# Attention output as full-array matmuls, with new buffer, load and filler orders, in a fused attention and FFN kernel on one Trainium2 core

## The chip, the cores and the metric

The kernel runs on one core of one Trainium2 chip. The metric is the device time of one execution in microseconds (us), as a median of several. All executions in this document are of the fast state. A profiled span is mostly 1.7 to 2.2 us shorter than the time reported for the same execution (2.7 for the profile of the kernel before, 3.2 at most), so spans are compared with spans and times with times. Several chips were used; each kernel was timed beside the kernel before on its own chip.

## The reference

Linear attention for 8 batches of 8 heads (576 tokens, head size 64), then a feed-forward layer on all 4608 tokens.

```python
q_s = exp(q - max(q, -1)); q_s = q_s / (sum(q_s, -1) + 1e-09)   # over head_dim
k_s = exp(k - max(k, 2));  k_s = k_s / (sum(k_s, 2) + 1e-09)    # over the sequence
kv  = einsum('bhsd,bhse->bhde', k_s, v)
x   = einsum('bhsd,bhde->bhse', q_s, kv)        # -> (4608, 512), heads side by side
h   = x @ w_in                                   # (512, 2048)
s   = sin(alpha * h)
g   = h + s * s / (alpha + 1e-09)
out = g @ w_out                                  # (2048, 512)
```

## The kernel before

The FFN runs in 9 tiles of 512 tokens, 0 to 8. A tile has 64 matmuls of 128x128x512 for h (16 groups of four) and 64 for o (four output chunks of 16). Between h and o, ACT takes the sine and mostly the square as well, and DVE combines the two into g. Attention of a batch is fitted between: batch 0 ahead of everything, batch 1 in tile 0's o, batch 2 in tile 1's o, batch 3 in tile 2's h, batches 4 to 7 in tiles 3 to 6. There, matmuls of the tile before's o serve as filler between the h groups.

The parts that the change touches; cuts are marked `# ...`.

```python
win_v = moe_w_in.rearrange("(ko ki) n -> ki ko n", ki=128)
def load_win(c):                          # 4 calls, 512 columns each
    nc.gpsimd.dma_start(out=win[:, :, c * 512:(c + 1) * 512], in_=win_v[:, :, c * 512:(c + 1) * 512])

def attn_out(b, ii, half, pool, eng):     # 4 calls for a batch
    qT, kt = A["qT", b], A["kvb", b]
    j0, j1 = XO[half]                     # 256 or 320 columns
    n = (j1 - j0) * P
    xp = pool.tile([128, 2, 512], F32, name="xp", tag="a")
    for x in range(2):
        r = slice(64 * x, 64 * x + 64)
        for e in range(2):
            nc.tensor.matmul(xp[64 * e:64 * e + 64, x, 0:n], kt[r, e, ii, :],
                             qT[r, j0:j1, ii, e * 64:(e + 1) * 64], start=True, stop=True)
    c0 = (J * b + j0) * P
    eng(xT[:, ii::2, c0:c0 + n], xp[:, :, 0:n])

def mm_h(t, ni, wide=None):
    # ...
    if wide and ni % 6 >= 4:
        hp = wide()                       # a bank lent by another pool
    else:
        hp = ps_h.tile([128, MF], F32, name="hp", tag="h")      # ring of 4
    # ... four matmuls

# tile 0's o: two chunks at a time, then batch 1's attention between the second two
os = o_pair(0, 0, [acc[:, 0], acc[:, 1]], [ACT_CP, ACT_CP])
# ...
os = o_pair(0, 2, [ps_h.tile(...) for _ in range(2)], [DVE_CP, ACT_CP])
take(os, 22)                              # issue 22 matmuls of it
q_transpose(1, 0, ps_e, ACT_CP)
# ...

ps_o = tc.tile_pool(name="ps_o", bufs=2, space=PSUM, ...)    # o's banks
ps_a = tc.tile_pool(name="ps_a", bufs=1, space=PSUM, ...)    # ONE slot for attention

def attn_back(b, n):
    if n == 0:
        kv_mm(b, 0, ps_a); kv_mm(b, 1, ps_a); kv_norm(b)
    elif 5 <= n < 9:
        attn_out(b, (n - 5) // 2, (n - 5) % 2, ps_a, DVE_CP)

for t in range(3, nT):
    b = t + 1 if t + 1 < B else None
    os = o_stream(t - 1)                  # copies a chunk out after its 16th matmul
    done = 0
    for ni in range(nN):
        hp = mm_h(t, ni)
        if b is not None:
            if ni == 4:
                q_transpose_dma(b)
            attn_back(b, ni - 5)
        s = sine(t, ni, hp, "A")
        combine(t, ni, hp, s)
        if b is not None and ni == 0:
            exp_q(b); exp_k(b); cast_v(b, [GP, GP]); norm_q(b, [GP])
            # ...
        want = 22 + 21 * ni // 8 if b is not None else 4 * (ni + 1)
        take(os, min(64, want) - done)    # filler
        done = min(64, want)
    take(os)
take(o_stream(nT - 1))                    # last chunk: a half copied by DVE, a half by ACT
```

The softmax here doesn't subtract the row's maximum and nothing guards it: scores larger than these inputs give would overflow.

## Time and profile before

| | before |
|---|---|
| time, median of 3 | 298.51 us (298.36 to 299.24) |
| profiled span | 296.6 us |
| PE busy | 94% |
| ACT, DVE, GpSimd busy | 77%, 63%, 29% |
| full-size FFN matmuls | 1152 x 0.216 = 248.6 us |

In a timeline line the first number is the start of a group, the second its duration, both in us; "x4" is the number of instructions, and a bracket gives the idle time before and who ended it. Matmuls overlap: a record lasts 0.379 us, but the next starts after 0.216. So the steps from start to start are read, and a wait is what a step has over (number x 0.216). The lines are in the prediction.

### The profile page before, as it was taken

Reading aid. Unit: us, or ns where it says so; the run is one execution under the profiler, and the core shown is the slowest. Engines: PE = TensorE matmul, PEld = TensorE weight load, DVE = VectorE, ACT = ScalarE, POOL = GpSimd, SP = SyncE. Lnnn points to the kernel's source line nnn. Section 1 sums busy time; section 2 is a strip of 40 time slices with the busy share of each in tenths; the row PEclk is TensorE's granted clock in tenths of the full one; section 3 lists DMA queues with packets and bytes.
Section 4 is the critical chain, followed back from the end, with each engine's and each line's share of the span. In section 5 each row is a group of like instructions: output and inputs, shape, how many; then the busy total and the mean of one; then the engine's idle time right before and its main releaser. Section 6 shows DMA issues by size and latency. Waiting matters only on the chain.

```text
span 296.6 us, 4313 instructions
## 1 busy us (share of the span) xinstructions
PE 278.1 (94%) x1595; PEld 127.0 (43%) x1624; DVE 185.5 (63%) x267; ACT 228.5 (77%) x320; POOL 84.6 (29%) x72
## 2 busy tenths in 40 slices
PE   1999998999898999999999999999999999999993
PEld 0444454444343444344444444444444444444441
DVE  2858664889648857764786568656874555555420
ACT  4788666999577899779987998799877777777400
POOL 0949453575755635001600052005000000000000
PEclk9999999999999999999999999999999999999999
DMA  7999979966789966109921894113411111111233
GB/s 263 278 206 200 314 266 298 398 245 184 162 135 368 390 203 128 39 6 331 289 53 23 277 291 98 39 35 69 83 35 35 38 35 35 35 39 43 48 86 71
DMA packets 35540, 45.76 MB, mean 154 GB/s; under 512 B 15792, under 2 KB 20416, under 8 KB 35520
## 3 DMA queue, kind: packets, MB, share of 16 engines
q1 hardware_dynamic: 29520, 34.09, 40.8%
q0 software_dynamic: 5888, 11.27, 15.2%
q8 instruction: 12, 0.20, 0.3%
q10 hardware_dynamic: 112, 0.14, 0.2%
q14 instruction: 8, 0.07, 0.1%
HBM read 36.71 MB, written 9.44 MB: 156 GB/s over the span
## 4 chain that ended last, share of the span: by engine, by line
PE 63%; ACT 15%; DVE 8%; DMA 4%; issue 4%; POOL 3%; SPq 1%; ACTq 0%
PE hp L215 28%; PE op L235 24%; ACT s L221 4%; DVE g L231 4%; ACT ke L111 3%; DMA st_v<-in_v_dram 3%; POOL s L225 2%; PE xp L198 2%; PE acc L235 2%; PE kvp L151 2%; PE hp L235 2%; ACT s L223 2%; ACT L221 2%; ACT L111 2%; ACT qe L111 2%
## 5 line engine op out<-in xcount | busy, mean ns | idle before, releaser
L231 DVE SCALAR_TENSOR_TENSOR g<-s,inva_sb,hp 128x512 bf16<-128x512 f32 x132 | 96.8, 745 | 68.5 <-ACT s L223 54.3
L215 PE MATMUL hp<-xT,win 128*128 128x512 bf16 x515 | 130.5, 379 | 2.7 <-DVE g L231 1.2
L235 PE MATMUL op<-wout,g 128*128 128x512 bf16 x498 | 125.7, 379 | 1.2 <-issue 0.6
L221 ACT ACTIVATE s<-hp,alpha_sb 128x512 f32<-128x512 f32 x132 | 88.9, 681 | 30.4 <-PE hp L215 23.2
L215 PEld LDWEIGHTS <-win 128*128 128x128 bf16 x576 | 55.7, 98 | 70.9 <-issue 4.3
L235 PEld LDWEIGHTS <-g 128*128 128x128 bf16 x576 | 54.1, 98 | 65.4 <-DVE g L231 0.4
L223 ACT ACTIVATE s<-s 128x512 f32<-128x512 f32 x112 | 70.5, 630 | 3.7
L141 POOL TENSOR_TENSOR qn<-qe,qs 128x2304 bf16<-128x2304 bf16 (+1 forms) x8 | 26.6, 3330 | 87.2 <-DVE qs L140 81.7
L225 POOL TENSOR_TENSOR s<-s 128x512 f32<-128x512 f32 x28 | 29.5, 1061 | 23.9 <-ACT s L221 23.8
L139 DVE TENSOR_REDUCE qs<-qe 128x18 f32<-128x1152 bf16 (+1 forms) x11 | 20.7, 1882 | 14.3 <-ACT qe L111 14.2
L241 DVE COPY o<-op 128x512 f32<-128x512 f32 x31 | 21.0, 677 | 10.1 <-PE op L235 10.1
L111 ACT ACTIVATE qe<-st_q 128x1152 bf16<-128x1152 f32 x16 | 17.9, 1155 | 4.8 <-DMA st_q<-in_q_dram 4.7
L111 ACT ACTIVATE ke<-st_k 128x1152 bf16<-128x1152 f32 x16 | 17.7, 1150 | 2.6 <-DMA st_k<-in_k_dram 2.6
L201 DVE CAST xT<-xp 128x512 bf16<-128x512 f32 (+1 forms) x24 | 17.8, 747 | 1.9 <-PE xp L198 1.5
L125 POOL CAST vb<-st_v 128x1152 bf16<-128x1152 f32 x14 | 16.1, 1178 | 8.8 <-DMA st_v<-in_v_dram 8.7
L198 PE MATMUL xp<-qT,kvb 64*64 64x256 bf16 (+1 forms) x128 | 9.7, 302 | 2.7 <-DVE xT L201 1.2
L247 ACT COPY o<-op 64x512 f32<-64x512 f32 x1 | 0.6, 581 | 14.0 <-DVE o L247 14.0
L198 PEld LDWEIGHTS <-kvb 64*64 64x64 bf16 x128 | 4.5, 103 | 13.9 <-issue 11.3
L151 PE MATMUL kvp<-vb,ke 64*128 64x130 bf16 x288 | 9.8, 216 | 0.6 <-DVE qT L181 0.6
L111 ACT ACT_TABLE_LOAD x7 | 9.0, 1283 | 1.3 <-PEq L477 1.2
L151 PEld LDWEIGHTS <-ke 64*128 64x128 bf16 x288 | 8.3, 93 | 3.7 <-issue 2.4
L201 ACT CAST xT<-xp 128x640 bf16<-128x640 f32 (+1 forms) x8 | 5.1, 653 | 5.9 <-PE xp L198 5.9
(52 smaller groups left out, 112.3 us busy)
## 6 DMA issues: line engine op xcount, KB each, us to landing
out_dram<-o SPq DMA_DIRECT2D x71, 128.0 KB, 2.4
st_q<-in_q_dram SPq DMA_DIRECT2D x5, 1152.0 KB, 6.8
st_k<-in_k_dram SPq DMA_DIRECT2D x5, 1152.0 KB, 9.3
st_v<-in_v_dram SPq DMA_DIRECT2D x5, 1152.0 KB, 10.4
st_k<-in_k_dram POOLq DMA_DIRECT2D x2, 1152.0 KB, 12.2
win<-in_moe_w_in_dram POOLq DMA_DIRECT2D x4, 512.0 KB, 8.3
wout<-in_moe_w_out_dram POOLq DMA_DIRECT2D x4, 512.0 KB, 16.3
st_q<-in_q_dram SPq DMA_DIRECT2D x2, 576.0 KB, 4.8
```

Of the source, the lines that this page charges most:

```text
L111: nc.scalar.activation(dst[:, :, ii * 128:(ii + 1) * 128].rearrange("p j (x d) -> p x j d", x=2), src[:, ii::2], AX.Exp)
L139: nc.vector.tensor_reduce(part, src, axis=AXL.X, op=ALU.add)
L141: engs[h].tensor_tensor(dst, src, part.unsqueeze(3).to_broadcast([128, J, w, D]), op=ALU.mult)
L151: nc.tensor.matmul(kvp[:, e, ii * 130:(ii + 1) * 130], ke[r, j, ii * 128:(ii + 1) * 128], vt[r, j, ii * 130:(ii + 1) * 130], start=(j == 0 ...
L201: eng(xT[:, ii::2, c0:c0 + n], xp[:, :, 0:n])
L215: nc.tensor.matmul(hp, win[:, ki, ni * 128:(ni + 1) * 128], xT[:, ki, t * MF:(t + 1) * MF], start=(ki == 0), stop=(ki == 3))
L221: nc.scalar.activation(s, hp, AX.Sin, scale=alpha_sb[:, ni:ni + 1])
L223: nc.scalar.activation(s, s, AX.Square)
L225: nc.gpsimd.tensor_tensor(s, s, s, op=ALU.mult)
L231: nc.vector.scalar_tensor_tensor(G[t][:, ni], in0=s, scalar=inva_sb[:, ni:ni + 1], in1=hp, op0=ALU.mult, op1=ALU.add)
L235: nc.tensor.matmul(acc, G[t][:, ni, j * 128:(j + 1) * 128], wout[:, ni, :], start=(ni == 0), stop=(ni == nN - 1))
L241: eng(o, acc)
```

## The change

Intent: make attention's output as cheap as its streaming time by giving TensorE whole 128x128 weights (kv of two heads, block-diagonal, the rest zeros written once). The rows of `w_in` are permuted to suit. Several waits are attacked as well: more o banks and a mixed order in tile 0, one more filler matmul in tiles 3 to 6, ACT for half of tile 2's evacuations, and a last chunk in two halves of 256 columns. The last `w_out` chunk is loaded after batch 1.

```diff
-    win_v = moe_w_in.rearrange("(ko ki) n -> ki ko n", ki=128)
+    win_v = moe_w_in.rearrange("(x c d) n -> x d c n", x=2, c=4)
-    def load_win(c):                      # 4 ranges of 512 columns
+    def load_win(c0, c1):                 # ranges (0,1), (1,2), (2,4)
+        n = slice(c0 * 512, c1 * 512)
+        for x in range(2):
+            nc.gpsimd.dma_start(out=win[64 * x:64 * x + 64, :, n], in_=win_v[x][:, :, n])
...
-            nc.vector.tensor_tensor(kt[r, :, i0:i1], src[r, :, :, x, 0:D],
+            nc.vector.tensor_tensor(kt[r, :, i0:i1, r], src[r, :, :, x, 0:D],
...
-        for x in range(2):
-            r = slice(64 * x, 64 * x + 64)
-            for e in range(2):
-                nc.tensor.matmul(xp[64 * e:64 * e + 64, x, 0:n], kt[r, e, ii, :],
-                                 qT[r, j0:j1, ii, e * 64:(e + 1) * 64], start=True, stop=True)
+        for e in range(2):
+            nc.tensor.matmul(xp[:, e, 0:n], kt[:, e, ii], qT[:, j0:j1, ii, e * 64:(e + 1) * 64],
+                             start=True, stop=True)
-        eng(xT[:, ii::2, c0:c0 + n], xp[:, :, 0:n])
+        eng(xT[:, 2 * ii:2 * ii + 2, c0:c0 + n], xp[:, :, 0:n])
...
-        if wide and ni % 6 >= 4:
+        if wide and ni % 6 in ((2, 3) if t == 0 else (4, 5)):
...   tile 0's o: o_pair twice -> o_quad once, on the four banks of h's ring
+        orders = [[(n, m) for p in (0, 2) for n in R for m in (p, p + 1)],
+                  [(n, m) for n in R for m in R], [(n, m) for n in R for m in R],
+                  [(n, m) for m in R for n in R]]
...   tile 0's squares: three on DVE (was two); exp_k(1) before the o matmuls (was among them)
...   batch 1: take(os, 44) before its transposes, then 2, 2, and 3 after each pair of outputs (was 22, 1, 1, 1)
...   opool (o's copies in SBUF) has 4 buffers (was 3)
...   tile 0 loads batch 1 after h groups 3, 6, 8 (was 4, 7, 10), w_out's last chunk after 11
...   batch 2: take(os, 26) before its outputs (was 24), then 2, 2, 1 (was 3, 3, 2)
-    def attn_back(b, n):
+    def attn_back(b, n, engs=(DVE_CP, DVE_CP)):
-            attn_out(b, (n - 5) // 2, (n - 5) % 2, ps_a, DVE_CP)
+            attn_out(b, (n - 5) // 2, (n - 5) % 2, ps_a, engs[n % 2])
-        attn_back(3, ni - 5)
+        attn_back(3, ni - 5, (DVE_CP, ACT_CP))
...
-            want = 22 + 21 * ni // 8 if b is not None else 4 * (ni + 1)
+            want = 23 + 21 * ni // 8 if b is not None else 4 * (ni + 1)
...
-    take(o_stream(nT - 1))
+    take(o_stream(nT - 1), 48)
+    for h in range(2):                    # last chunk in two halves of 256 columns
+        ...
+        evac_o(nT - 1, 3, acc, DVE_CP, cols, (nc.sync, nc.scalar))
```

More of the change, by code (lines that the diff above doesn't have):

```diff
@@ L60 @@
     spool = ctx.enter_context(tc.tile_pool(name="spool", bufs=4))
-    opool = ctx.enter_context(tc.tile_pool(name="opool", bufs=3))
+    opool = ctx.enter_context(tc.tile_pool(name="opool", bufs=4))
     PSUM = bass.MemoryType.PSUM
@@ L72 @@
     inva_sb = singles.tile([128, nN], F32, name="inva_sb")
+    kbd = [singles.tile([128, 2, 2, 128], BF16, name=f"kbd{n}") for n in range(2)]
     vb = [singles.tile([128, J, 4 * 65], BF16, name=f"vb{n}") for n in range(2)]
@@ L98, in load_batch @@
         load("v", v, b)
-    def load_win(c):
-        nc.gpsimd.dma_start(out=win[:, :, c * 512:(c + 1) * 512], in_=win_v[:, :, c * 512:(c + 1) * 512])
+    def load_win(c0, c1):
+        n = slice(c0 * 512, c1 * 512)
+        for x in range(2):
+            nc.gpsimd.dma_start(out=win[64 * x:64 * x + 64, :, n], in_=win_v[x][:, :, n])
     def load_wout(c):
@@ L156, in kv_norm @@
     def kv_norm(b, i0=0, i1=2):
-        if i0 == 0:
-            A["kvb", b] = att2.tile([128, 2, 2, D], BF16, name="kvb")
-        kt, m = A["kvb", b], i1 - i0
+        kt, m = kbd[b % 2], i1 - i0
         kvr = small.tile([128, 2, 2, 2], F32, name="kvr")[:, :, 0:m]
@@ L190, in attn_out @@
     def attn_out(b, ii, half, pool, eng):
-        qT, kt = A["qT", b], A["kvb", b]
+        qT, kt = A["qT", b], kbd[b % 2]
         j0, j1 = XO[half]
@@ L236, in mm_o, with evac_o @@
                          start=(ni == 0), stop=(ni == nN - 1))
-    def evac_o(t, j, acc, eng, last=False):
-        if not last:
-            o = opool.tile([128, dm], F32, name="o")
-            eng(o, acc)
+    def evac_o(t, j, acc, eng, cols=None, queues=None):
+        cols = cols or slice(0, dm)
+        o = opool.tile([128, dm], F32, name="o")
+        eng(o[:, cols], acc)
         for hf in range(2):
-            r = slice(64 * hf, 64 * hf + 64)
             blk = t * BPT + 2 * j + hf
-            if last:
-                o = opool.tile([128, dm], F32, name="o")
-                (nc.vector.tensor_copy, nc.scalar.copy)[hf](o[r], acc[r])
-            (nc.sync, nc.scalar)[hf if last else 0].dma_start(out=out_v[blk // J, blk % J], in_=o[r])
+            (queues or (nc.sync, nc.sync))[hf].dma_start(out=out_v[blk // J, blk % J][:, cols],
+                                                         in_=o[64 * hf:64 * hf + 64, cols])
     ACT_CP, DVE_CP = nc.scalar.copy, nc.vector.tensor_copy
@@ L265 @@
     for n in range(2):
+        nc.vector.memset(kbd[n], 0.0)
         nc.vector.memset(vb[n].rearrange("p j (i c) -> p j i c", i=4)[:, :, :, D:D + 1], 1.0)
@@ L289 @@
         norm_q(0, [GP, V])
-        for c in range(4):
-            load_win(c)
-        for c in range(4):
+        for c0, c1 in ((0, 1), (1, 2), (2, 4)):
+            load_win(c0, c1)
+        for c in range(3):
             load_wout(c)
@@ L316, in flush, with o_quad @@
             combine(*lag.pop(0))
-    def o_pair(t, j0, accs, engs):
-        for ni in range(nN):
-            for n in range(2):
-                mm_o(t, j0 + n, ni, accs[n])
+    def o_quad(t, accs, engs):
+        R = range(4)
+        orders = [[(n, m) for p in (0, 2) for n in R for m in (p, p + 1)],
+                  [(n, m) for n in R for m in R], [(n, m) for n in R for m in R],
+                  [(n, m) for m in R for n in R]]
+        for c in R:
+            for n, m in orders[c]:
+                mm_o(t, m, 4 * c + n, accs[m])
+                if c == 3 and n == 3:
+                    evac_o(t, m, accs[m], engs[m])
                 yield
-        for n in range(2):
-            evac_o(t, j0 + n, accs[n], engs[n])
-        yield
     def take(it, n=1000):
@@ L337, in lent @@
             return ps_e.tile([128, 2, MF], F32, name="hh", tag="a")[:, 0]
-        late = {4: ("q", q, 1, True), 7: ("k", k, 1, False), 10: ("v", v, 1, True)}
+        late = {3: ("q", q, 1, True), 6: ("k", k, 1, False), 8: ("v", v, 1, True)}
         for ni in range(nN):
-            h_slot(0, ni, SQ[ni], lag, lent)
+            h_slot(0, ni, "PAPDPAPADPAPPDAP"[ni], lag, lent)
             flush(lag, 1)
@@ L345 @@
                 load(name, x, b, halves=hv, eng=GP)
+            if ni == 11:
+                load_wout(3)
         flush(lag, 0)
@@ L349 @@
         norm_q(1, [GP, V])
-        acc = ps_e.tile([128, 2, dm], F32, name="acc", tag="a")
-        os = o_pair(0, 0, [acc[:, 0], acc[:, 1]], [ACT_CP, ACT_CP])
-        take(os, 32)
         exp_k(1)
-        take(os)
         cast_v(1, [GP, GP])
@@ L357 @@
             load(name, x, 2, eng=GP)
-        os = o_pair(0, 2, [ps_h.tile([128, dm], F32, name="hp", tag="h") for _ in range(2)], [DVE_CP, ACT_CP])
-        take(os, 22)
+        accs = [ps_h.tile([128, dm], F32, name="hp", tag="h") for _ in range(4)]
+        os = o_quad(0, accs, [DVE_CP, ACT_CP, DVE_CP, ACT_CP])
+        take(os, 44)
         q_transpose(1, 0, ps_e, ACT_CP)
         nc.scalar.activation(zero, zero, AX.Sin)
-        take(os, 1)
+        take(os, 2)
         q_transpose(1, 1, ps_e, DVE_CP)
-        take(os, 1)
+        take(os, 2)
         kv_mm(1, 0, ps_e)
@@ L371 @@
             attn_out(1, ii, 1, ps_e, ACT_CP)
-            take(os, 1)
+            take(os, 3)
         take(os)
@@ L392, in o_stream @@
                 if ni == nN - 1:
-                    evac_o(t, j, acc, eng, last=(t == nT - 1 and j == 3))
+                    evac_o(t, j, acc, eng)
                 yield
@@ L412 @@
     norm_q(3, [GP])
-    take(os, 24)
+    take(os, 26)
     for n in range(4):
         attn_out(2, n // 2, n % 2, ps_a, ACT_CP)
-        take(os, (3, 3, 2, 1000)[n])
+        take(os, (2, 2, 1, 1000)[n])
     q_transpose_dma(3)
     load_batch(4)
-    def attn_back(b, n):
+    def attn_back(b, n, engs=(DVE_CP, DVE_CP)):
         if n == 0:
@@ L460 @@
         take(os)
-    take(o_stream(nT - 1))
+    take(o_stream(nT - 1), 48)
+    for h in range(2):
+        cols = slice(h * 256, h * 256 + 256)
+        acc = ps_o.tile([128, 256], F32, name="op", tag="o")
+        for ni in range(nN):
+            nc.tensor.matmul(acc, G[nT - 1][:, ni, 384:512], wout[:, ni, cols], start=(ni == 0), stop=(ni == nN - 1))
+        evac_o(nT - 1, 3, acc, DVE_CP, cols, (nc.sync, nc.scalar))
 _INS = ['q', 'k', 'v', 'moe_w_in', 'moe_w_out', 'moe_alpha']
```

## The prediction

> **What bounds the kernel now.** I read the busy shares first, then the row of TensorE (PE) in the 40 slices, then the costly groups, and last the timeline and the waits at the places where PE is not full. From the page:
>
> ```profile
> PE 278.1 (94%) x1595; PEld 127.0 (43%) x1624; DVE 185.5 (63%) x267; ACT 228.5 (77%) x320; POOL 84.6 (29%) x72
> ...
> PE   1999998999898999999999999999999999999993
> ...
> L215 PE MATMUL hp<-xT,win 128*128 128x512 bf16 x515 | 130.5, 379 | 2.7 <-DVE g L231 1.2
> L235 PE MATMUL op<-wout,g 128*128 128x512 bf16 x498 | 125.7, 379 | 1.2 <-issue 0.6
> ...
> L198 PE MATMUL xp<-qT,kvb 64*64 64x256 bf16 (+1 forms) x128 | 9.7, 302 | 2.7 <-DVE xT L201 1.2
> L247 ACT COPY o<-op 64x512 f32<-64x512 f32 x1 | 0.6, 581 | 14.0 <-DVE o L247 14.0
> L198 PEld LDWEIGHTS <-kvb 64*64 64x64 bf16 x128 | 4.5, 103 | 13.9 <-issue 11.3
> ```
>
> PE is the bound from 17 us on. One matmul record lasts 379 ns, but they overlap: four take 0.86 us from the first start to the start of the next group, 0.216 us each. The FFN has 9 tiles x (64 + 64) = 1152 of them (weight loads: 576 + 576), 248.6 us of a 296.6 us span. About 17 us of head and 5 us of tail come on top, and some 26 us of attention matmuls and waits. Only those can shrink. The last two rows name two targets: the weight loads of attention's output (13.9 us of idle charged to them), and a final copy on ACT that waits for a final copy on DVE.
>
> The timeline of PE in one middle tile shows what an attention output costs:
>
> ```profile
> 119.69 1.03 PE L215 MATMUL hp<-xT,win 128*128 128x512 bf16 x4
> 120.65 0.30 PE L198 MATMUL xp<-qT,kvb 64*64 64x256 bf16 x4
> 120.89 0.82 PE L235 MATMUL op<-wout,g 128*128 128x512 bf16 x3
> 121.54 1.03 PE L215 MATMUL hp<-xT,win 128*128 128x512 bf16 x4
> 122.50 0.33 PE L198 MATMUL xp<-qT,kvb 64*64 64x320 bf16 x4
> 122.76 0.60 PE L235 MATMUL op<-wout,g 128*128 128x512 bf16 x2
> ```
>
> Four full matmuls from 119.69 would let the next start at 119.69 + 0.863 = 120.55. The 64x64 group starts at 120.65, so 0.09 goes on entering. Its four start within 0.01 us of each other (they do run side by side), yet the next full matmul starts only at 120.89. The call costs 120.89 - 120.55 = 0.33 us; the 320-column one 122.76 - 122.40 = 0.355.
>
> The end, and one recurring wait, from the timeline:
>
> ```profile
> 291.86 0.68 DVE L247 COPY o<-op 64x512 f32<-64x512 f32 x1 [2.76 <-PE op L235]
> 292.58 0.58 ACT L247 COPY o<-op 64x512 f32<-64x512 f32 x1 [14.04 <-DVE o L247]
> 293.19 0.55 ACTq L248 DMA_DIRECT2D out_dram<-o  x1
> ...
> 111.34 1.02 PE L215 MATMUL hp<-xT,win 128*128 128x512 bf16 x4 [0.21 <-DVE g L231]
> ...
> 142.04 1.02 PE L215 MATMUL hp<-xT,win 128*128 128x512 bf16 x4 [0.16 <-DVE g L231]
> ```
>
> The two half copies run one after the other. The wait at 142.04 comes once in each of tiles 3 to 6: ACT does the next batch's exponentials, the four PSUM banks of h fill up, and PE has used its 22 filler matmuls. From start to start it is 0.32 us (0.37 at 111).
>
> **What the Trainium skill says.** "TensorEngine Tiling (Array Packing)", Key Properties: changing the tiling mode, not just the tile, drains TensorE. The trace agrees: 0.09 us in and about 0.12 out beyond the streaming time. "TensorE: Matmul & The Clock Gate", Back-to-back issue gap: about N/2.4 + 2.5 ns at the full clock, 216 ns for N=512. The trace has 0.216 and the granted clock is 1.00 nearly throughout, so I use it for N=256 (0.109) and N=320 (0.136). "PSUM — Partial Sum Buffer", on bank collisions: different quadrants of one bank may be accessed together. Yet the trace shows ACT waiting for DVE on the two halves of one bank, so the kernel as built serialises them. "SBUF — State Buffer", Who interferes with whom: a DVE instruction with two SBUF inputs contends with GpSimd reads. The DVE squares (L227) average 1.12 us, one took 1.53, beside 0.75 for a combine.
>
> **The change part by part.**
>
> (1) Attention's output as full-array matmuls. A call of 4 small ones becomes 2 full ones: 2 x 0.109 = 0.218 against 0.33, and 2 x 0.136 = 0.272 against 0.355. Savings 0.11 and 0.08, two of each per batch, 0.39 us per batch. The zeros are written once, in a stretch before 4.3 us where DVE only waits. The chain of a call gets longer: the second matmul starts 0.11 to 0.14 later instead of 0.01, so an evacuation that somebody waits for comes 0.1 later.
>
> (2) Filler 22 to 23. One more matmul in front of the recurring wait cuts it from 0.32 to about 0.10. With (1), each of tiles 3 to 6 saves 0.39 + 0.22 = 0.61, if ACT keeps up. It was idle 3.5 of the 30.7 us period (my sum of its gaps), so it should. **4 x 0.61 = 2.4 us.** Tiles 7 and 8 have no attention and no stall: nothing.
>
> (3) Tail. The last chunk runs as two halves of 256 columns, 32 x 0.109 = 3.49 against 16 x 0.216 = 3.45: +0.04. The first half is copied under the second. After it comes one DVE copy of 128x256, estimated 0.41 (0.68 for 512 columns, of which 0.53 is one column per cycle at 0.96 GHz; the rest fixed), and two stores go out at once. Before, 0.68 + 0.04 + 0.58 lay between the matmul and the last store: 1.30 against 0.41 + 0.04. **-0.85 us.**
>
> (4) Tile 0 to the start of tile 1 (17.0 to 50). PE's steps between starts show these waits: 0.71 before the last h group (a bank that DVE frees late), about 0.5 before batch 1's kv, 0.23 after it ("issue"), 0.42 between attention outputs, 0.2 at tile 1's start. About 2.1 in all. The new order gives o four banks of h's ring, keeps three matmuls instead of one between attention outputs and leaves four behind: that covers the last two (0.6) and (1) saves 0.39. Against that: the third DVE square puts 1.1 us more on DVE, which sets the pace there (16 combines of 0.7 plus squares fill 20 to 35 us). Stepping it by hand I get waits of about 0.5 at h's end and 0.5 at o's third and fourth banks. Loads: w_in and w_out go through one queue, which moves its 4096 rows of 1 KB at about 200 per us, from 12 to 33 us; batch 1's q, k and v follow at 3 us each (q's first exponential waits until 36.1). With 512 rows taken out, they land some 2.5 us earlier, q at 34, when ACT is just done with its sines. The last w_out chunk then lands near 42.5, needed near 45. **-0.8 us**, the least sure term.
>
> (5) Batch 2's attention (tile 1's output). It waits for the transposing transfer: 0.80 before the first output at 78.11. Two more filler matmuls fill that wait but do not bring the data. From there, one PSUM slot and an evacuation by ACT set the pace: 78.11 to 82.32, each evacuation starting 0.35 after its matmul. With the longer call, 4 x 0.1 = +0.4. The new w_in row order lets the next h run two of its four matmuls before the last evacuation instead of one: -0.2. **+0.2.**
>
> (6) Tile 2. Its 0.93 us wait before the second output (DVE behind on combines) stays, since DVE still evacuates the first. Half of the evacuations go to ACT. **-0.2.**
>
> (7) Head: v's landing near 12 us sets it and is untouched; full-array kv needs both halves normalised, +0.1 to 0.2, given back by the row order at the first h. 0.
>
> Sum: -2.4 - 0.85 - 0.8 + 0.2 - 0.2 = -4.05; 298.5 - 4.05 = 294.4.
>
> **Rivals.**
> (a) ACT or DVE becomes the bound in tiles 3 to 6 and the 0.39 turns into waits. For: ACT 77% busy, the recurring wait is already ACT's chain of 11.5 us. Against: after it PE spends 1.4 us per h block, ACT 1.24, so ACT catches up and later waits for PE. Then about 296.
> (b) New waits in tile 0 and batch 1 (a w_out chunk that lands too late, GpSimd squares queued behind load issues, the transposes waiting for q at the earlier place) eat all of (4) and more: 295.5 to 296.5.
> (c) The reordering works fully: no wait in tile 0 and batch 1 (-2.4 instead of -0.8), and batch 2 no longer waits: 292 to 292.5.
> (d) The shorter w_in/w_out queue is worth nothing in itself, as loads were hidden: ACT's 1.45 us wait at 36 lay beside full PE work. I take this as true; only the rearranged matmuls use it.
>
> **Range and chances.** Terms 2 and 3 are firm to some 0.5 us together; 4 to 6 may be off by 1.5. Range 292.2 to 296.4. Two per cent is 292.5: only (c) reaches it. Faster by over 2%: 0.11; within: 0.88; slower: 0.01.
>
> **What would show it right or wrong.** In the middle tiles, an attention output should be two matmuls of 128x128, the next matmul starting 0.22 or 0.27 after the first, with no 0.09 in front; the period, 30.7 now (112.36 to 143.06 between kv groups), should be 30.1. If the period stays, (a) is right. At the end one DVE copy of about 0.4 us, two stores side by side, no ACT copy. Tile 1's first h near 49, not 49.9. The gap from batch 2's first output to tile 2's second h group should not shrink. The prediction is wrong if the period moves by less than 0.4, or if tile 1 starts over 1.5 us earlier or later than now.

## The result and the profile after

| | before | after |
|---|---|---|
| time, median of 4 | 298.66 us (298.36 to 299.24) | 296.80 us (296.58 to 297.66) |
| ratio | 1 | 0.9941 (95%: 0.9915 to 0.9967) |
| profiled span | 296.61 us | 294.80 us |

The change makes the kernel 0.6% faster, which is within 2%. The median lies 0.4 us above the range, and less than half of the predicted 4.05 us came. A ratio here is the mean time of one kernel's fast runs over that of the other's of the same rounds, so it is not quite the ratio of the medians quoted.

From the page of the changed kernel (busy shares, the PE row of the 40 slices, and groups of instructions with busy time and mean ns, then the idle time before them):

```profile
PE 279.5 (95%) x1576; PEld 132.4 (45%) x1576; DVE 185.9 (63%) x270; ACT 228.1 (77%) x320; POOL 84.6 (29%) x73
...
PE   2999999999799999999999999999999999999994
...
L215 PE MATMUL hp<-xT,win 128*128 128x512 bf16 x520 | 129.7, 379 | 0.3
L235 PE MATMUL op<-wout,g 128*128 128x512 bf16 x496 | 123.8, 379 | 0.0
...
L198 PE MATMUL xp<-qT,kbd 128*128 128x256 bf16 (+1 forms) x64 | 12.4, 285 | 4.2 <-ACT xT L201 1.8
```

The idle time before h's and o's matmuls has all but gone (2.7 to 0.3 and 1.2 to 0.0 us). That before attention's output has grown instead, from 2.7 to 4.2 us over half as many instructions. One slice of the PE row is down to 7: the eleventh, at 74 to 81 us, which is batch 2.

Stage by stage, between the first weight loads of each kind in the two traces, the third column being a second trace of the changed kernel:

| stage | before | after | after, again | change (of the first trace) | predicted |
|---|---|---|---|---|---|
| start to tile 0's h | 16.97 | 17.61 | 17.18 | +0.64 | 0 |
| tile 0's h to tile 1's o | 46.55 | 45.74 | 46.28 | -0.81 | -0.8 |
| tile 1's o to tile 2's h (batch 2) | 17.94 | 18.86 | 18.83 | +0.92 | +0.2 |
| tile 2's h to its o | 18.94 | 18.22 | 18.22 | -0.72 | -0.2 |
| tile 2's o to tile 3's kv | 11.89 | 11.93 | 11.94 | +0.04 | 0 |
| kv to kv, tiles 3 to 6 (three periods) | 92.10 | 91.08 | 91.07 | -1.02 | -1.83 |
| kv in tile 6 to PE's end | 87.44 | 87.14 | 87.13 | -0.30 | -0.57 |
| PE's end to the end of the span | 4.79 | 4.22 | 4.53 | -0.57 | -0.85 |

In the last column the 23rd filler matmul is counted where it now runs: it brings 0.22 into the stage before the first kv, where it cuts the wait by as much, and is gone from the stage after the last kv. These changes add up to -1.8 us. Three terms were missed by 0.6 us or more: the middle tiles, batch 2, and the head.

The timeline of PE in a middle tile, after:

```profile
119.77 1.03 PE L215 MATMUL hp<-xT,win 128*128 128x512 bf16 x4
120.63 0.38 PE L198 MATMUL xp<-qT,kbd 128*128 128x256 bf16 x2
120.85 0.81 PE L235 MATMUL op<-wout,g 128*128 128x512 bf16 x3
121.50 1.03 PE L215 MATMUL hp<-xT,win 128*128 128x512 bf16 x4
122.36 0.43 PE L198 MATMUL xp<-qT,kbd 128*128 128x320 bf16 x2
122.63 0.59 PE L235 MATMUL op<-wout,g 128*128 128x512 bf16 x2
123.06 1.03 PE L215 MATMUL hp<-xT,win 128*128 128x512 bf16 x4
124.34 0.38 PE L198 MATMUL xp<-qT,kbd 128*128 128x256 bf16 x2 [0.26 <-DVE xT L201]
```

The form is as cheap as computed. An output starts 0.86 after the four h matmuls in front of it, with no 0.09 for entering, and the next matmul follows 0.22 (120.63 to 120.85) or 0.27 later. But the third output starts 1.28 after 123.06 instead of 0.86: a wait of 0.42. Before, the same step had a wait of 0.11 beside the 0.09 for entering (timeline of PE, before):

```profile
123.21 1.03 PE L215 MATMUL hp<-xT,win 128*128 128x512 bf16 x4
124.27 0.30 PE L198 MATMUL xp<-qT,kvb 64*64 64x256 bf16 x4
```

The timelines of DVE in the same stretch, after and then before, say why:

```profile
121.58 0.68 DVE L201 CAST xT<-xp 128x512 bf16<-128x512 f32 x1
122.21 0.75 DVE L231 SCALAR_TENSOR_TENSOR g<-s,inva_sb,hp 128x512 bf16<-128x512 f32 x1
122.88 0.69 DVE L241 COPY o<-op 128x512 f32<-128x512 f32 x1
123.48 0.82 DVE L201 CAST xT<-xp 128x640 bf16<-128x640 f32 x1
```

```profile
122.80 0.68 DVE L241 COPY o<-op 128x512 f32<-128x512 f32 x1
123.41 0.81 DVE L201 CAST xT<-xp 128x640 bf16<-128x640 f32 x1
```

DVE works without a gap here. The second output's evacuation, which frees the only slot of attention's PSUM pool, starts at 123.48, 0.85 after the matmuls it reads have made way for others (122.63), because the copy of a finished o chunk stands in front of it. It ends at 124.30, and the third output starts at 124.34. In the trace of before, DVE had the same unbroken sequence and the third output started 0.05 after that evacuation, as it does in the changed kernel. PE had lost its time in the drains, and now loses it waiting.

The timeline around batch 2's first output, before and then after:

```profile
78.11 0.30 PE L198 MATMUL xp<-qT,kvb 64*64 64x256 bf16 x4 [0.80 <-DMA qT<-qn]
```

```profile
71.78 5.79 PE L235 MATMUL op<-wout,g 128*128 128x512 bf16 x26
78.62 0.38 PE L198 MATMUL xp<-qT,kbd 128*128 128x256 bf16 x2 [1.06 <-DMA qT<-qn]
78.84 0.59 PE L235 MATMUL op<-wout,g 128*128 128x512 bf16 x2
79.67 0.43 PE L198 MATMUL xp<-qT,kbd 128*128 128x320 bf16 x2 [0.24 <-ACT xT L201]
```

PE has two more matmuls to fill with, and still waits longer, as the transposed q comes 0.5 us later (78.62 against 78.11). The outputs after it then wait for ACT's evacuations, as predicted.

The head, before and then after, and the tail after:

```profile
6.29 4.90 PE L281 MATMUL warm<-qe,identb 128*128 128x512 bf16 x14 [1.99 <-ACT qe L111]
```

```profile
6.07 6.13 PE L279 MATMUL warm<-qe,identb 128*128 128x512 bf16 x14 [2.82 <-ACT qe L114]
...
286.92 3.66 PE L468 MATMUL op<-wout,g 128*128 128x256 bf16 x32
288.87 0.42 DVE L241 COPY o<-op 128x256 f32<-128x256 f32 x1 [1.06 <-PE op L468]
290.62 0.42 DVE L241 COPY o<-op 128x256 f32<-128x256 f32 x1 [1.32 <-PE op L468]
```

The same 14 warm-up matmuls took 4.90 us in one trace and 6.13 in the other. The records of the granted clock show full speed from 9.80 us in the trace before, from 12.09 after, and from 9.92 in the second trace after. The tail is as predicted: one copy of 0.42 us after the last matmul and two stores.

### The profile page after: what moved, and what is told of

It reads as the page before. It is cut to its first block, busy times and chain, and to the rows that moved or that the text cites. A ratio compares the mean times of both kernels' runs of the same rounds, so it can differ in the third digit from the quotient of the medians.

```text
span 294.8 us, 4250 instructions
## 1 busy us (share of the span) xinstructions
PE 279.5 (95%) x1576; PEld 132.4 (45%) x1576; DVE 185.9 (63%) x270; ACT 228.1 (77%) x320; POOL 84.6 (29%) x73
## 4 chain that ended last, share of the span: by engine, by line
PE 75%; DVE 9%; ACT 5%; POOL 3%; DMA 3%; issue 2%; ACTq 0%; SPq 0%
PE op L235 31%; PE hp L215 30%; PE hp L235 4%; DVE g L231 3%; PE xp L198 3%; PE warm L279 2%; POOL s L225 2%; DVE xT L201 2%; ACT s L221 2%; PE kvp L154 2%; DMA qT<-qn 2%; DMA st_q<-in_q_dram 1%; DVE o L241 1%; ACT xT L201 1%; PE op L468 1%
## 5 line engine op out<-in xcount | busy, mean ns | idle before, releaser
L231 DVE SCALAR_TENSOR_TENSOR g<-s,inva_sb,hp 128x512 bf16<-128x512 f32 x130 | 95.3, 746 | 65.1 <-ACT s L223 52.3
L235 PE MATMUL op<-wout,g 128*128 128x512 bf16 x496 | 123.8, 379 | 0.0
L221 ACT ACTIVATE s<-hp,alpha_sb 128x512 f32<-128x512 f32 x130 | 87.8, 682 | 27.0 <-PE hp L215 23.0
L241 DVE COPY o<-op 128x512 f32<-128x512 f32 (+1 forms) x33 | 21.9, 663 | 14.2 <-PE op L235 11.8
L128 POOL CAST vb<-st_v 128x1152 bf16<-128x1152 f32 x14 | 16.5, 1210 | 7.9 <-DMA st_v<-in_v_dram 7.9
L201 DVE CAST xT<-xp 128x512 bf16<-128x512 f32 (+1 forms) x22 | 16.5, 753 | 2.8 <-PE xp L198 2.7
L198 PE MATMUL xp<-qT,kbd 128*128 128x256 bf16 (+1 forms) x64 | 12.4, 285 | 4.2 <-ACT xT L201 1.8
L235 PE MATMUL hp<-wout,g 128*128 128x512 bf16 x64 | 15.1, 379 | 0.4 <-DVE g L231 0.3
L198 PEld LDWEIGHTS <-kbd 128*128 128x128 bf16 x64 | 6.0, 97 | 12.9 <-issue 5.7
L201 ACT CAST xT<-xp 128x512 bf16<-128x512 f32 (+1 forms) x10 | 6.3, 638 | 7.0 <-PE xp L198 6.9
L279 PE MATMUL warm<-qe,identb 128*128 128x512 bf16 x19 | 7.5, 562 | 2.8 <-ACT qe L114 2.8
```

Source lines behind the costliest of these rows:

```text
L198: nc.tensor.matmul(xp[:, e, 0:n], kt[:, e, ii], qT[:, j0:j1, ii, e * 64:(e + 1) * 64], start=True, stop=True)
L201: eng(xT[:, 2 * ii:2 * ii + 2, c0:c0 + n], xp[:, :, 0:n])
L221: nc.scalar.activation(s, hp, AX.Sin, scale=alpha_sb[:, ni:ni + 1])
L231: nc.vector.scalar_tensor_tensor(G[t][:, ni], in0=s, scalar=inva_sb[:, ni:ni + 1], in1=hp, op0=ALU.mult, op1=ALU.add)
L235: nc.tensor.matmul(acc, G[t][:, ni, j * 128:(j + 1) * 128], wout[:, ni, :], start=(ni == 0), stop=(ni == nN - 1))
L241: eng(o[:, cols], acc)
```

## The experiments

Every run was correct and in the fast state. "This / before" are the medians of the same rounds. Except where it says "before", each edit is made to the changed kernel.

### First round: is it the form, the wait behind it, or chance?

The theory: in tiles 3 to 6 the array form saves what was computed, but DVE's order gives it back at the third output. The rivals: the form itself costs something not seen, or the trace was an unlucky one.

**r1_after_again.** The changed kernel once more, no edit.

> The changed kernel once more, for a second trace and a tighter time. Theory: two of the microseconds that differ between the two traces are luck of one execution. The clock was released at 12.09 us in the changed kernel's trace and at 9.80 us in the one before, and the first h matmul stood at 17.64 against 17.00; and one of the 16 completions of batch 2's transposing transfer came at 78.49 while the other 15 were in by 77.84. Then in a second trace the release lies elsewhere between 9 and 13 us, h's start follows it, and the late completion does not recur in the same place. Rival: both belong to the program (the memsets, the six w_in transfers, the place of an instruction fetch), and come again within 0.1 us. Time: ratio to the kernel before 0.994.

296.66 / 298.67 us, ratio 0.9939 (0.9922 to 0.9955). The stages of this trace stand in the table above. The head's +0.64 shrinks to +0.21 and tile 0's gain from 0.81 to 0.27. Batch 2 (+0.89), tile 2 and the middle tiles repeat within 0.03. So the theory was half right: the head was partly chance, but the late completion in batch 2's transfer came again (78.57, the others by 77.93), as the rival had it; e7 takes it up. In tile 0, this trace shows a wait that the late head of the first one had hidden:

```profile
24.68 1.67 PE L215 MATMUL hh<-xT,win 128*128 128x512 bf16 x7 [0.40 <-DMA win<-in_moe_w_in_dram]
```

The ninth h group (columns 1024 onward) waits for the merged range of `w_in`, of which all 1024 columns must land first. No step of the prediction had it.

**e1_array_only.** The kernel before, with the block-diagonal kv, the full-array matmuls and the rows of `w_in` alone.

> The kernel before with the block-diagonal kv and the w_in rows that go with it, and nothing else. Theory (absorbed): in the middle tiles the third attention output already waited about 0.1 us for DVE to evacuate the second, because DVE copies an o chunk first; the cheaper matmuls only lengthen that wait to about 0.4. The period of a middle tile goes from 30.70 to some 30.6, batch 2 loses 0.3, ratio 0.997 to 1.001. Rival (as I predicted): the period falls by 0.39 or more, to 30.3, and the ratio is 0.993 to 0.995.

299.03 / 298.67 us, ratio 1.0013 (1.0005 to 1.0021). Alone, the array form is worth nothing and costs a trace of time. Its period is 30.57 against 30.70; batch 2 and the head (h at 17.50) give that back.

**e2_quadrants_back.** The changed kernel with the four 64x64 matmuls and the old row order (loaded in the same ranges).

> The changed kernel with the four 64x64 matmuls and the old w_in row order put back, all else as changed. Theory (absorbed): it loses little, because what the array form saves is waited away: ratio to the kernel before 0.993 to 0.997, period of a middle tile about 30.45 against 30.36. Rival: the array form carries most of the gain, and the ratio rises to 0.998 to 1.002.

296.40 / 298.67 us, ratio 0.9931 (0.9913 to 0.9948). This is no worse than the changed kernel (0.9939). The period is 30.48 with quadrants and 30.36 with the array form: 0.12 a tile instead of the 0.39 that was computed. So all of the gain of this change came from its other parts.

**e3_evac_alt.** ACT for two of the four evacuations in tiles 3 to 6.

```diff
-    def attn_back(b, n, engs=(DVE_CP, DVE_CP)):
+    def attn_back(b, n, engs=(DVE_CP, ACT_CP)):
```

> The changed kernel with one edit: in the middle tiles the second and fourth attention outputs are evacuated by ACT instead of DVE. Theory (absorbed): the 0.42 us wait before the third output, in each of tiles 3 to 6, falls below 0.1, the period goes from 30.36 to about 30.0, and the whole gains 4 x 0.35 = 1.4 us on the changed kernel: ratio to the kernel before near 0.989. Rival: the wait has another cause or moves to the next place (ACT then runs its sines later, and h waits for a bank): ratio stays 0.993 to 0.995.

299.47 / 298.67 us, ratio 1.0026 (1.0016 to 1.0037). A miss, and by a slip of mine: the outputs are counted from n = 5, so `engs[n % 2]` gives the first and third to ACT, not the second and fourth that were meant. The second evacuation stayed on DVE and came later still. The timeline of PE, the third output:

```profile
156.86 0.38 PE L198 MATMUL xp<-qT,kbd 128*128 128x256 bf16 x2 [0.96 <-DVE xT L201]
```

The wait there is 1.12 from start to start, and the period 31.06. The slip bears on tile 2 as well: the prediction read the same index in the same way, and held that DVE still evacuates the first output there. In fact ACT does.

### Second round: move the wait, and single out batch 2 and tile 0

**e6_act_second.** The edit that e3 had meant: `engs=(ACT_CP, DVE_CP)`, second and fourth evacuations on ACT.

> What e3_evac_alt was meant to be: the engines stand the other way round, for the outputs are numbered from 5. Its edit gave the first and third output to ACT and left the second on DVE behind the o copy, and the wait before the third grew to 1.12 us. Here the second and fourth go to ACT. Theory (DVE's copy holds the second evacuation): the wait before the third output falls from 0.42 to under 0.15, period about 30.1, ratio 0.990 to 0.991. Rival (ACT's sines, delayed by the evacuations, hold up DVE's combines and with them h's banks or the first evacuation): period 30.4 or more, ratio 0.994 or worse.

297.08 / 298.50 us, ratio 0.9948 (0.9935 to 0.9962). The wait before the third output is gone. But another came before the fourth, 0.55 from start to start, and the period is 30.49, longer than 30.36. ACT's copy delays its sines, so DVE's combine comes late (DVE is idle 1.25 us for ACT before it) and its evacuation with it. The rival was right here. The timeline of PE, the fourth output:

```profile
157.11 0.43 PE L198 MATMUL xp<-qT,kbd 128*128 128x320 bf16 x2 [0.39 <-DVE xT L201]
```

**e4_filler25.** Two more filler matmuls: `want = 25 + 21 * ni // 8`.

> The changed kernel with two more filler matmuls before the recurring wait in the middle tiles (25 for 23), nothing else. With 25, the o chunk that ends at matmul 48 ends one h block earlier, so DVE copies it before the first attention output and no longer between the second one and its evacuation. Theory (the wait of 0.42 us before the third output comes from that copy on DVE): it goes, and so does the rest of the recurring wait (0.10): period 30.36 to 29.9, 4 x 0.45 = 1.8 us, ratio to the kernel before 0.988. Rival (the wait comes from the one PSUM slot and the evacuation itself, whoever stands in front): only 0.1 per tile, ratio 0.992 to 0.993.

297.28 / 298.50 us, ratio 0.9954 (0.9940 to 0.9968), period 30.40. The recurring wait for ACT's chain is covered, and yet nothing is gained: a wait of 0.555 stands before the second output. The filler count also sets where a chunk of o ends, and thus where its copy stands in DVE's queue. The third chunk ends at the 48th o matmul. With 23 (`23 + 21*ni//8` passes 48 at ni = 10) the copy stands between the first and second evacuation. With 25 it is reached at ni = 9, right ahead of the first evacuation. Part of this kernel's time is a late head besides (h at 18.41 in its trace).

**e5_win_four.** `w_in` in the four ranges (0,1), (1,2), (2,3), (3,4) again.

> The changed kernel with w_in's third and fourth column ranges loaded by two pairs of transfers instead of one pair. In four of five traces with the merged pair, the ninth h group of tile 0 (the first that needs it) starts 0.56 to 1.2 us late, though the profile names no releaser there. Theory (it waits for the merged pair, which lands only when both ranges are in): that step closes to 0.22; the gain is at most 0.6 us as DVE's combines limit what follows: ratio 0.992 to 0.994. Rival (a PSUM bank or DVE holds it): the step stays.

296.55 / 298.50 us, ratio 0.9933 (0.9920 to 0.9945). The ninth h group no longer waits, and tile 0's h to tile 1's o takes 45.73, against 46.28 in r1. The ratio, against r1's 0.9939, moved by less than its interval. What there is to be had differs from execution to execution: from start to start, the ninth group waits 0 to 1.75 us in the nine traces with the merged range (none in the first, 0.56 in r1, 1.58 in e8, 1.75 in e12), and not at all in the five of the changed kernel with four ranges. (The expectation says that the profile names no releaser; r1's timeline, above, does. And of the four traces with the merged range then at hand, three had the wait.)

**e7_pool_pad.** Four tiny writes on GpSimd at the start, of a tile that nobody reads. They do no work, but shift the stream of instructions; the tile also takes a place in SBUF.

```diff
+    pad = singles.tile([128, 1], F32, name="pad")
+    for _ in range(4):
+        nc.gpsimd.memset(pad, 0.0)
```

> The changed kernel with four tiny GpSimd memsets in its idle time at the start; they do no work and only move later instructions of that engine in its stream. In the four traces of kernels where an 8 KB instruction fetch falls into the last packets of batch 2's transposing transfer (76.8 to 78.0 us), one of its 16 completions comes 0.64 to 0.65 us after the others; in the two where it falls elsewhere (74.4, 79.0) all are in within 0.03. Theory (the fetch delays that completion, and GpSimd's stream places it): the fetch moves by a few us, all 16 completions come within 0.1, and tile 2's h starts about 0.6 us earlier relative to tile 1's o; ratio 0.991 to 0.993. Rival (the late completion has to do with the transfer's own load): it stays at 0.65, ratio 0.994. If the fetch doesn't move, the run decides nothing.

295.67 / 298.50 us, ratio 0.9910 (0.9895 to 0.9925). The reason for trying it: the transfer that transposes batch 2's q ends in 16 completions, and the records of DMA packets and semaphores show (us):

```
                  issue   15th, 16th completion    8 KB instruction fetch starts
before            73.30   77.96  77.97             79.00
e1_array_only     74.01   78.85  78.86             74.43
after             73.13   77.84  78.49             77.32 (0.31 long)
after, again      73.24   77.93  78.57             77.40 (0.31 long)
e7_pool_pad       73.48   77.54  77.55             72.45 (0.69 long), next at 85.06
```

Where the fetch falls on the last packets of the transfer, the last completion comes 0.64 to 0.65 us after the others, and PE starts only then. "DMA: Bandwidth & Descriptors", section Why a DMA increments its semaphore by 16 and not by 1, in the Trainium skill says that the engines of a transfer finish independently and the semaphore counts each; this trace agrees, with one straggler of 16. The kernel before had the same in tile 5's transfer (180.34, then 181.16, with a fetch at 179.59) and in tile 6's (209.86, then 211.46, with one of 16 KB at 209.40). There nobody was waiting. "Runtime: NRT & Kernel Launch", section Instruction fetch mechanics, says that a sequencer fetches its next block through a DMA queue of its own, at a cost that is mostly hidden; if the fetch is the cause, here it was not, by 0.65 us. With the stream shifted, the timeline of PE has:

```profile
71.77 5.79 PE L235 MATMUL op<-wout,g 128*128 128x512 bf16 x26
77.68 0.38 PE L198 MATMUL xp<-qT,kbd 128*128 128x256 bf16 x2
```

The first output starts at 77.68 instead of 78.62, and tile 1's o to tile 2's h takes 17.93 instead of 18.83 to 18.86. Of these 0.9 us, 0.65 is the straggler. The rest is a transfer that was faster from its first packets on (4.07 from issue to last completion, 4.71 up to the 15th in the changed kernel) though issued 0.36 later, and why is open. The padding does more than move the fetch: batch 4's transfer, which no fetch touches, is faster with it too (3.88 up to the 15th completion against 4.60).

The kernel has six such transfers, so the 16 traces hold 96. In 14 the last completion is 0.64 us or more late, and in each of these a fetch starts 0.46 to 0.75 us before the 15th: ten times batch 2's (8 KB, 0.64 to 0.67 late), twice batch 6's (8 KB, 0.82) and twice batch 7's (16 KB, 1.56 and 1.60). Of the other 82 none is more than 0.05 late; only two of them have a fetch in the last microsecond before the 15th completion (16 KB, batch 5 in e12 and e13). Batch 2's has no fetch there in e7, e10, e11 and e13, which have the padding, nor in the kernel before and e1, which have not. So a late fetch stands with every straggler, and once in a while without one. That it is the cause is inferred from this; the kept records do not tell which DMA engine completes late.

### Third round: enough filler, a better order in tile 0, and all together with and without the array form

**e8_filler28.** `want = 28 + 21 * ni // 8`, which puts the copy two h blocks ahead of the first output.

> The changed kernel with 28 filler matmuls for 23 in the middle tiles. With 25 the wait did not go, it moved: the o copy then stood on DVE in front of the first output's evacuation, and the wait of 0.56 us came before the second output. With 28 the chunk of 48 ends two h blocks before the first output, where DVE has gaps of 0.7 us. Theory (a copy of o on DVE in front of an evacuation, whichever, holds the single PSUM slot): no wait over 0.15 before any of the four outputs, no recurring wait, period 30.36 to 29.9, ratio 0.987 to 0.989. Rival (PE is simply ahead of ACT's and DVE's chain by then, and the wait comes somewhere in any case): period 30.3 or more, ratio 0.993 or worse.

296.22 / 299.00 us, ratio 0.9906 (0.9887 to 0.9924), period 30.25 to 30.32, which is the rival's. No output waits, but there is a new wait of 0.48 from start to start, seen in the timeline of PE at the 33rd matmul of o:

```profile
170.83 0.38 PE L235 MATMUL op<-wout,g 128*128 128x512 bf16 x1 [0.32 <-DVE o L241]
```

That matmul needs the bank of o's first chunk. The chunk's copy stands on DVE behind the row sums of the next batch's exponentials. With 28 the 33rd matmul comes in h block 2 (28 + 5 = 33); with 27 it would come in block 3.

**e9_win_order.** Four ranges of `w_in`, and in tile 0's o the first two accumulators get 16 matmuls before the other two start.

```diff
+        steps = [(c, n, m) for p in (0, 2) for c in (0, 1) for n in R for m in (p, p + 1)]
+        steps += [(2, n, m) for n, m in orders[2]] + [(3, n, m) for n, m in orders[3]]
```

> The changed kernel with w_in's four ranges loaded apart (as in e5_win_four, where the late ninth h group went) and with tile 0's first 16 output matmuls all in the first two accumulators, so that the third and fourth, whose banks DVE frees late (0.27 and 0.44 us of waits in every trace of this family), come 8 matmuls later. Theory: both waits go, 0.7 us; some 0.2 of it comes back in front of the transposes or the kv matmuls, which wait for q and v; tile 0's o to tile 1's o 32.1 to 31.6 us, ratio 0.991 to 0.992. Rival (the stage ends with loads or with ACT, not with these banks): 32.0, ratio 0.993 or more.

295.81 / 299.00 us, ratio 0.9891 (0.9872 to 0.9910). Tile 0's o to tile 1's o takes 31.38 instead of 32.10, since the waits of 0.27 and 0.44 for the banks of the third and fourth accumulator, which every earlier trace of the changed kernel shows, are gone. Tile 0's h to tile 1's o takes 45.0, against 46.55 before.

**e10_all_array** and **e11_all_quadrants.** 28 fillers, e9's edits, e7's padding, and batch 2's evacuation split between ACT and DVE, one bank each; the first with the array form and the second with quadrants. This tests the form where no output waits for the slot.

> All findings together on the changed kernel: 28 filler matmuls, w_in in four, the new order of tile 0's output, the four GpSimd memsets that moved the instruction fetch, and batch 2's evacuations split between ACT and DVE, one PSUM bank each. Expected if the parts add up: middle tiles 4 x 0.45, fetch 0.6, tile 0 0.5, batch 2's chain 4 x 0.25: 3.9 us below the changed kernel, ratio 0.980 to 0.983, and a version that beats both kernels. Rival (each gain becomes the next wait): 0.987 or more.

> The same as e10_all_array but with the four 64x64 matmuls and the old w_in rows. This asks what the array form is worth once nothing waits behind it. Theory (its 0.39 us per batch was real and only absorbed): this is slower than e10 by 0.3 to 0.4 us in each of tiles 3 to 6, 1.2 to 1.6 in all, ratio 0.004 to 0.006 above. Rival (the array form is worth nothing in any schedule): within 0.001 of e10.

293.97 and 295.25 / 299.00 us, ratios 0.9839 (0.9811 to 0.9866) and 0.9872 (0.9850 to 0.9894). The periods are 30.32 and about 30.75, and both keep e8's wait at the 33rd matmul: the array form is worth 0.43 a tile here, near the computed 0.39 (1.28 us in all, where 1.2 to 1.6 was expected), while behind the changed kernel's wait it was worth 0.12. The split was a miss: batch 2's stage took 18.49 instead of e7's 17.93. ACT and DVE worked one after the other (timelines of e10, second output):

```profile
78.13 0.43 ACT L252 CAST xT<-xp 128x320 bf16<-128x320 f32 x1 [0.98 <-PE xp L198]
78.59 0.49 DVE L253 CAST xT<-xp 128x320 bf16<-128x320 f32 x1 [0.98 <-ACT xT L252]
```

DVE was idle and waited for ACT: in the trace, each of its four halves waits for the semaphore that ACT's half sends. So the program as built orders the two, as it did the two half copies at the end of the kernel before. (The first output, which e13's expectation quotes, does not show it: DVE was busy there with a copy of o.)

### Fourth round: the filler count that the queue order asks for

By the two counts found above, 27 should be the one: the copy of the third chunk at ni = 8 (27 + 21 = 48), two blocks ahead of the first output, and the 33rd matmul after block 2 (27 + 5 = 32).

**e12_filler27.** `want = 27 + 21 * ni // 8`, nothing else.

> The changed kernel with 27 filler matmuls in the middle tiles. In the trace with 28 no wait stood before the outputs any more, but 0.48 us before matmul 33 of o: the third accumulator needs the bank of the first, whose copy stands on DVE behind the next batch's row sums, which wait for ACT's exponentials. 28 reaches matmul 33 one h block early; 27 reaches it after that block, and still puts the copy after matmul 48 ahead of the outputs. Theory (copies of o that stand on DVE behind or in front of attention's work cause every one of these waits): no wait over 0.15 in the middle tile, period 29.85 (1152/9 = 128 matmuls x 0.2158 = 27.62, kv 1.22, outputs 0.98), 2 us below the changed kernel, ratio 0.986 to 0.988. Rival (PE is ahead of a chain through ACT whose length sets the period): the wait appears a fourth time, period 30.2 or more, ratio 0.991 or more.

295.80 / 299.41 us, ratio 0.9881 (0.9867 to 0.9896), period 29.84. The timelines of DVE and of PE:

```profile
152.03 0.68 DVE L241 COPY o<-op 128x512 f32<-128x512 f32 x1
152.88 0.75 DVE L231 SCALAR_TENSOR_TENSOR g<-s,inva_sb,hp 128x512 bf16<-128x512 f32 x1 [0.16 <-ACT s L223]
153.54 0.69 DVE L201 CAST xT<-xp 128x512 bf16<-128x512 f32 x1
```

```profile
155.02 1.03 PE L215 MATMUL hp<-xT,win 128*128 128x512 bf16 x4
155.88 0.38 PE L198 MATMUL xp<-qT,kbd 128*128 128x256 bf16 x2
```

The copy now stands before the first output's evacuation, with a combine between, and the third output starts 0.86 after its h group: no wait. It is PE alone that sets the period. (In tile 0 this trace has the longest wait for the merged range of `w_in`, 1.75 us.)

**e13_best.** e12 with e9's order and ranges and e7's padding, without the split.

> e10_all_array with 27 for 28 and without the split evacuation of batch 2, which cost time: its trace shows DVE's half starting only when ACT's was done (76.78 + 0.37, then 77.18), so each evacuation took 0.8 instead of 0.6 us, and tile 1's o to tile 2's h rose to 18.49 us where the kernel with the moved fetch alone had 17.93. Expected if the theory of e12 holds: 4 x 0.48 + 0.56 = 2.5 us below e10, ratio 0.974 to 0.977, faster than both kernels. Rival: ratio 0.981 or more.

292.57 (292.10 to 293.01) / 299.41 us, ratio 0.9772 (0.9755 to 0.9790): faster than both kernels. Against the first trace of the changed kernel, the span is 4.0 us shorter (290.79). The middle tiles from tile 2's o to PE's end give 2.2 of it, batch 2's stage 1.2 and tile 0 to tile 1's o 0.7; head and tail cancel to 0.1.

## Why the prediction was right or wrong

**The step that failed** is "With (1), each of tiles 3 to 6 saves 0.39 + 0.22 = 0.61, if ACT keeps up." Both savings were sized right, and the condition named the wrong engine. The array form costs 0.22 and 0.27 us a call, and the recurring wait fell from 0.32 to 0.10. But a period fell by 0.34, not 0.61 (and in tile 3 the wait before kv fell from 0.37 to 0.19 only): the third output's wait grew from 0.11 to 0.42 and took back 0.31. What keeps it waiting is neither engine's total load (DVE is busy 63%), but one slot of PSUM and the order of five instructions in DVE's queue. That order was in the trace of before, with an unbroken DVE. Rival (a) came nearest, with "about 296" and "ACT or DVE becomes the bound", but gave DVE no queue. e1, e2, e4, e6, e10, e11 and e12 show it: behind the wait the form is worth 0.12 a tile, with the wait covered 0.43, and with a filler count that moves the copy the period is 29.84.

**Batch 2** (predicted +0.2, came +0.92). The longer chain was right in kind: the steps between outputs grew from 0.98, 1.13, 0.98 to 1.05, 1.22, 1.05, which is 0.23 of the 0.4 booked. What was missing is the straggling completion of the transposing transfer, 0.65 us, which no reading of the trace before would have put into this place. In all six traces without a fetch on its last packets it is absent; that the fetch causes it is inferred.

**Tile 0 to tile 1** (predicted -0.8, came -0.81 and -0.27). That the first number is so near is luck, for its parts were not. The waits foreseen at o's third and fourth banks came (0.27 and 0.44 for 0.5); the one foreseen at h's end shows in neither trace. The 0.39 booked for the form in batch 1 did not come: there outputs go back to back in pairs and share the entry, so the two pairs cost 0.47 and 0.49 us before and 0.49 each after. The wait at tile 1's start, read as 0.2, was 0.41 (the missing record of that tile lies elsewhere, at 55.75), and it went. The wait for the merged range of `w_in` was not foreseen; in the first trace the late head hid it. e9 shows what the stage gives without them.

**Tile 2** (predicted -0.2, came -0.72). I booked nothing for the form there and misread the index. ACT has the first evacuation, so the wait of 0.93 before the second output did not stay: it is 0.71 with the array form, and 0.52 with quadrants in e2's trace. That wait gives 0.22, the form's own saving 0.39, and 0.14 came at the stage's start, where before h's second matmul waited for batch 2's last evacuation. With quadrants the stage takes 18.35, only 0.13 more: here too the form gives most of its saving back to a wait.

**The head** (predicted 0, came +0.64 and +0.21). Over all traces, full clock came between 9.4 and 12.1 us, and tile 0's h started at 16.9 to 17.9 with the array form (18.41 in one), 16.5 to 17.0 with quadrants (three traces). The form may cost a little there, since both halves of kv must be normalised first; beside the chance of when the clock was granted, these traces do not give its size. **The tail** (predicted -0.85, came -0.57 in one trace): two traces of the old tail have 4.79 and 5.00, and 14 of the new one 3.70 to 4.53, mean 4.09, so -0.81 on average. That step holds. (The 0.41 predicted for the last copy came as 0.42. Its working is cut above; an estimate from this trace, with DVE at 0.68 us for 512 columns and 0.82 for 640, gives 0.40 for 256.)

Another reading was wrong without effect: the 0.23 after kv that the prediction lists as an "issue" wait is a matmul missing from the records, as steps of 0.216 there show.

## What to carry to other kernels

A saving on the bound engine counts only up to the next event that it needs from another engine. So follow the buffer that the cheaper work needs, to the queue of the engine that frees it, and count the instructions in that queue; here one copy of 0.68 us ate most of a saving of 0.39 per tile. A filler count is a schedule for every engine behind it: 25 and 28 each left a wait of about 0.5 us, 27 none, and simple counting of where a chunk ends told which. Before crediting or blaming a change for half a microsecond in one transfer, take a second trace and look at the completions one by one.

## What the Trainium skill lacked or had wrong

- "Runtime: NRT & Kernel Launch" calls the cost of crossing an instruction block mostly hidden. "DMA: Bandwidth & Descriptors" has a general rule that fits, in Queues, rings and completion order: a semaphore increment lands only after every earlier write of its DMA engine, across its queues. But neither names an instruction fetch as what can hold up a transfer, or gives a size. Here all 14 stragglers of 96 transfers had a fetch 0.46 to 0.75 us before the 15th completion, and were 0.64 to 0.82 us late with 8 KB and 1.56 to 1.60 with 16 KB; two transfers with a late fetch were on time.
- "TensorEngine Tiling (Array Packing)" says that a mode switch drains TensorE, without a figure. Here it is 0.09 us on entering and about 0.12 beyond the streaming time on leaving. Doing without it (full-array matmuls for quadrants) is worth 0.43 us a tile where no output waits, and 0.12 where an evacuation sets the pace.
- No page that I read says how a missing matmul record looks: as an "issue" wait of 0.16 us, with the step from start to start a multiple of 0.216.
